# Attention over cached windows on one core: groups of four caches with K stationary, against groups of eight caches with q and P stationary

## The chip, the cores and the metric

One NeuronCore of a Trainium2 chip. The metric is the device time of one execution, in microseconds (us). Unless a range is given, a time is the median of the runs. "Fast" and "slow" are states of a run: a run more than 1.5% above the fastest of its kernel counts as slow, and a single run of a kernel has the state "unknown". TensorE is PE in the profile (its weight loads: PEld), VectorE DVE, ScalarE ACT, GpSimd POOL, SyncE SP. The "clock" is the TensorE clock that was granted, 1.0 being full speed.

## The reference

A decode step: layer norm, attention of one new token over the last 1024 keys of a cache, and a gated FFN whose output multiplies the attention's.

```python
xn = layernorm(x)                                   # x: [8, 1, 512] bf16
q  = (xn @ wq) -> [8, 32 heads, 1, 128]             # wq: [512, 4096]
k  = repeat(k_cache[:, :, 3072:4096], 4)            # caches: [8, 8 kv heads, 4096, 128]
v  = repeat(v_cache[:, :, 3072:4096], 4)
p  = softmax(q @ k^T * 128**-0.5)
s  = (p @ v) @ wo                                   # wo: [4096, 512]
g  = silu((gelu(xn @ w_gate) * (xn @ w_up)) @ w_down)   # F = 1792
out = x + s * g
```

There are 64 windows (8 batches by 8 kv heads) of 256 KB for K and as many for V: 33.6 MB. The weights bring the bytes read to 47.5 MB. The output is so close to x that a wrong order of keys passes the comparison with the reference; only wrong softmax sums failed it (relative error 0.03).

## The kernel before

A group is 4 caches of one kv head (a cache: the window of one batch). K comes as a 1 MB tile: partition 4r+i holds rows of cache i, 8 KB (32 keys) each, with r from 0 to 31. PE transposes K in blocks of 8, VectorE copies the block to SBUF, and K^T is the stationary operand for the scores (the one that the weight loads, PEld, read; the other is the moving one), so that the scores stand with the keys on partitions and 16 query columns beside them. An exp per cache i masks the rows of the other caches through its bias. V is stationary for the values.

```python
I = 4; R = 128 // I; C = 1024 // R                  # 4 caches, 32 rows, 32 keys a row
def load_cache(src, g):
    t = slot()                                      # ring of 21 slots of [128, 8 KB]
    rows = src[b0 : b0 + I, hkv, win0:Sk, :].rearrange("i (r c) d -> r i (c d)", c=C)
    nc.sync.dma_start(out=t, in_=rows)
...
# score_block, 8 of these, N = 16:
nc.tensor.matmul(sc[g][:, s * CB + c, :], kT[n][:, c * P : (c + 1) * P], qT_all[:, hkv, b0 : b0 + I, :], ...)
# once per group, 4 exps of 128 elements a partition:
for i in range(I):
    nc.scalar.activation(out=pT[g][:, :, i * rep : (i + 1) * rep],
                         in_=sc[g][:, :, i * rep : (i + 1) * rep],
                         func=ACT.Exp, bias=diag[:, i : i + 1], scale=inv_sqrt_dh)
# sums by a matmul with ones and a reduction on VectorE; values, 32 of these, N = 16:
nc.tensor.matmul(oT[g], v_t[g][:, c * Dh : (c + 1) * Dh], pT[g][:, c, :], ...)
```

(The load order is K0, w_q, then K and V in turn, FFN, w_o.)

The softmax here doesn't subtract the row's maximum and nothing guards it: scores larger than these inputs give would overflow.

Of the kernel before, what the change touches and what calls it, by code (L numbers as in the profile page):

```python
# [7 lines left out]
ACT = mybir.ActivationFunctionType  # L8
ALU = mybir.AluOpType
AX = mybir.AxisListType  # L10
BF16 = mybir.dt.bfloat16
# [4 lines left out]
def kernel(  # L16
# [13 lines left out]
    nc = tc.nc  # L30
# [14 lines left out]
    I = 4  # L45
    R = P // I
    C = W // R
    NG = Hkv * B // I
    GPH = B // I
    IR = I * rep  # L50
    CB = 8
    NB = C // CB
    SLOT = C * Dh
# [9 lines left out]
    ring = ctx.enter_context(tc.tile_pool(name="ring", bufs=21))  # L63
    consts = ctx.enter_context(tc.tile_pool(name="consts", bufs=1))
    persist = ctx.enter_context(tc.tile_pool(name="persist", bufs=1))
    kT_pool = ctx.enter_context(tc.tile_pool(name="kT_pool", bufs=4))
    p_pool = ctx.enter_context(tc.tile_pool(name="p_pool", bufs=3))
    small = ctx.enter_context(tc.tile_pool(name="small", bufs=3))
    ps_kT = ctx.enter_context(tc.tile_pool(name="ps_kT", bufs=3, space=bass.MemoryType.PSUM))
    ps_sc = ctx.enter_context(tc.tile_pool(name="ps_sc", bufs=2, space=bass.MemoryType.PSUM))  # L70
    ps_m = ctx.enter_context(tc.tile_pool(name="ps_m", bufs=2, space=bass.MemoryType.PSUM))
    ps_s = ctx.enter_context(tc.tile_pool(name="ps_s", bufs=1, space=bass.MemoryType.PSUM))
# [8 lines left out]
    def slot():  # L81
        return ring.tile([P, SLOT], BF16, name="slot")

    k_t, v_t, wo_t = {}, {}, {}
    wq_t, wg_t, wu_t, wd_t = [], [], [], []

    def load_cache(src, g):
        t = slot()
        hkv, b0 = g // GPH, (g % GPH) * I
        rows = src[b0 : b0 + I, hkv, win0:Sk, :].rearrange("i (r c) d -> r i (c d)", c=C)  # L90
        nc.sync.dma_start(out=t, in_=rows)  # L91
        return t
# [6 lines left out]

    def load_wq():  # L100
        for k in range(NDC):
            t = slot()
            nc.sync.dma_start(out=t, in_=A_wq[k * P : (k + 1) * P, :])  # L103
            wq_t.append(t)

    def load_ffn():
        for dst, src in ((wg_t, B_w_gate), (wu_t, B_w_up)):
            for a in range(2):
                t = slot()
                nc.sync.dma_start(  # L110
                    out=t[:, 0 : 2 * F],
                    in_=src[a * 2 * P : (a + 1) * 2 * P, :].rearrange(
                        "(p k) f -> p (k f)", k=2
                    ),
                )
                dst.append(t[:, 0 : 2 * F].rearrange("p (k f) -> p k f", k=2))
        JH = JF // 2
        wd = B_w_down.rearrange("(p j) d -> p j d", j=JF)
        for a in range(2):
            t = slot()[:, 0 : JH * D].rearrange("p (j d) -> p j d", j=JH)  # L120
            nc.sync.dma_start(out=t, in_=wd[:, a * JH : (a + 1) * JH, :])
            wd_t.extend(t[:, j, :] for j in range(JH))

# [20 lines left out]
    for m in range(NM):  # L144
# [9 lines left out]
    ones_pp = consts.tile([P, P], BF16, name="ones_pp")  # L154
    nc.vector.memset(ones_pp, 1.0)
# [3 lines left out]
    sel = consts.tile([P, R, I], FP32, name="sel")  # L159
    nc.gpsimd.memset(sel, 0.0)  # L160
    nc.gpsimd.affine_select(
        out=sel, in_=sel, compare_op=ALU.not_equal, fill=1.0, base=0,
        pattern=[[-I, R], [-1, I]], channel_multiplier=1,
    )
    diag = consts.tile([P, I], FP32, name="diag")
    nc.vector.tensor_reduce(
        out=diag, in_=sel.rearrange("p r i -> p i r"), axis=AX.X, op=ALU.add
# [30 lines left out]
    xq_sb = persist.tile([P, P], BF16, name="xq_sb")  # L198
    nc.gpsimd.memset(xq_sb, 0.0)
    for q in range(NQ):  # L200
        nc.scalar.dma_start(
            out=xq_sb[32 * q : 32 * q + B, :], in_=x_flat[:, q * P : (q + 1) * P]
        )


# [22 lines left out]
    s_ps = ps_s.tile([P, P], FP32, name="s_ps")  # L228
    nc.vector.memset(s_ps, 0.0)

    def transpose_x():
        t = ps_m.tile([P, 2, NDC, B], BF16, name="m_ps")
        for k in range(NDC):
            nc.tensor.transpose(t[:, 0, k, :], xhat[:, k * P : (k + 1) * P], ident[0:B, 0:B])  # L234
        xp = xhat.rearrange("b (a p k) -> b a k p", a=2, k=2)
        for a in range(2):
            for k in range(2):
                nc.tensor.transpose(t[:, 1, 2 * a + k, :], xp[:, a, k, :], ident[0:B, 0:B])
        nc.vector.tensor_copy(out=xnT_sb[:, :, 0:B], in_=t[:, 0])
        nc.vector.tensor_copy(out=xpT_sb[:, :, 0:B], in_=t[:, 1])  # L240


    def project_q():
        NW = rep * Dh
        q_sb = persist.tile([P, Hkv // NQ, NW], BF16, name="q_sb")
        q_ps = [ps_m.tile([P, NW], FP32, name="m_ps") for n in range(Hkv // NQ)]
# [28 lines left out]
    kT, sc, pT, oT = {}, {}, {}, {}  # L275

    def transpose_block(n):
        g, s = n // NB, n % NB
        t_ps = ps_kT.tile([P, CB * P], BF16, name="kT_ps")
        for c in range(CB):  # L280
            cc = s * CB + c
            nc.tensor.transpose(  # L282
                t_ps[:, c * P : (c + 1) * P], k_t[g][:, cc * Dh : (cc + 1) * Dh], ident
            )
        kT[n] = kT_pool.tile([P, CB * P], BF16, name="kT")
        nc.vector.tensor_copy(out=kT[n], in_=t_ps)  # L286

    def score_block(n):
        g, s = n // NB, n % NB
        hkv, b0 = g // GPH, (g % GPH) * I  # L290
        if s == 0:
            sc[g] = ps_sc.tile([P, C, IR], FP32, name="sc_ps")
        for c in range(CB):
            nc.tensor.matmul(  # L294
                sc[g][:, s * CB + c, :],
                kT[n][:, c * P : (c + 1) * P],
                qT_all[:, hkv, b0 : b0 + I, :],
                start=True,
                stop=True,
            )  # L300
        if s == NB - 1:
            pT[g] = p_pool.tile([P, C, IR], BF16, name="pT")
            for i in range(I):
                nc.scalar.activation(  # L304
                    out=pT[g][:, :, i * rep : (i + 1) * rep],
                    in_=sc[g][:, :, i * rep : (i + 1) * rep],
                    func=ACT.Exp,
                    bias=diag[:, i : i + 1],
                    scale=inv_sqrt_dh,
                )  # L310

    recip = {}

    def sum_group(g):
        sums_ps = ps_m.tile([P, C, IR], FP32, name="m_ps")
        nc.tensor.matmul(sums_ps, ones_pp, pT[g], start=True, stop=True)  # L316
        sums = small.tile([P, IR], FP32, name="sums")
        nc.vector.tensor_reduce(  # L318
            out=sums, in_=sums_ps.rearrange("p c m -> p m c"), axis=AX.X, op=ALU.add
        )  # L320
        recip[g] = small.tile([P, IR], FP32, name="recip")
        nc.vector.reciprocal(out=recip[g], in_=sums)  # L322

    def value_block(g, s):
        if s == 0:
            sum_group(g)
            oT[g] = ps_m.tile([P, IR], FP32, name="m_ps")
        for c in range(s * CB, (s + 1) * CB):
            nc.tensor.matmul(  # L329
                oT[g],  # L330
                v_t[g][:, c * Dh : (c + 1) * Dh],
                pT[g][:, c, :],
                start=(c == 0),
                stop=(c == C - 1),
            )
        if s == NB - 1:
            hkv, b0 = g // GPH, (g % GPH) * I
            nc.vector.tensor_tensor(  # L338
                out=oT_all[:, hkv * rep : (hkv + 1) * rep, b0 : b0 + I].rearrange(
                    "p j i -> p i j"  # L340
                ),
                in0=oT[g].rearrange("p (i j) -> p i j", i=I),
                in1=recip[g].rearrange("p (i j) -> p i j", i=I),
                op=ALU.mult,
            )

    oE, wide_t = {}, {}
# [32 lines left out]
    def project_out(m):  # L380
        for e in range(HS):
            for q in range(NQ):
                nc.tensor.matmul(  # L383
                    s_ps[32 * q : 32 * q + B, :],
# [11 lines left out]
    def ffn_up():  # L396
        gu_ps = [ps_m.tile([P, JQ * P], FP32, name="m_ps") for w in range(2)]
        for w, wt in enumerate((wg_t, wu_t)):
            for k in range(NDC):
                cols = wt[k // 2][:, k % 2, :].rearrange("x (p j) -> x j p", j=JF)  # L400
# [30 lines left out]
    def ffn_down():  # L431
        f_ps = ps_m.tile([P, P], FP32, name="m_ps")
        nc.vector.memset(f_ps, 0.0)
        for j in range(JF):
            r = j // JQ
            for q in range(NQ):
# [3 lines left out]
                    wd_t[j][:, q * P : (q + 1) * P],  # L440
# [12 lines left out]
    LA, LAG = 2, 6  # L453
    N = NG * NB
    transpose_x()
    for n in range(LA):
        transpose_block(n)
    project_q()
    for n in range(N + LAG):
        if n + LA < N:  # L460
            transpose_block(n + LA)
        if n < N:
            score_block(n)
        if n >= LAG:
            g, s = (n - LAG) // NB, (n - LAG) % NB
            value_block(g, s)
            GM = HS // rep * GPH
            if g % GM == 0 and g > 0:
                if s == 0:
                    expand_out(g // GM - 1)  # L470
                if s == 3:
                    select_out(g // GM - 1)
# [10 lines left out]
    nc.vector.tensor_tensor(out=tmp, in0=s_ps, in1=g_sb, op=ALU.mult)  # L483
# [37 lines left out]
```

## Time and profile before

| | before |
|---|---|
| time, median of 4 runs | 123.24 us (123.22 to 123.33) |
| span of the profiled run | 121.1 us |
| DMA rate in the slices of the loop | 414 to 434 GB/s |
| PE, DVE, ACT busy | 71%, 60%, 19% |
| mean clock | 0.85 |

The first lines are from the profile page before: the span, busy time with shares and instruction counts, then the span cut in 40 slices (DMA: busy tenths of the 16 engines; GB/s: what they moved).

```profile
span 121.1 us, 4123 instructions
PE 86.0 (71%) x1856; PEld 71.1 (59%) x1856; DVE 72.3 (60%) x150; ACT 22.6 (19%) x70; POOL 2.4 (2%) x15
...
DMA  3999999999999999999999999999999999999820
GB/s 84 387 430 430 430 427 417 419 430 425 425 427 427 425 414 422 430 419 430 425 427 422 422 417 430 422 425 422 425 433 418 422 414 434 416 430 423 341 88 5
```

DMA is at 9 tenths in all slices but the first and the last three; over the span, no compute engine is above 71%. The queue lines of the page (packets, MB, share of 16 engines' span) and its chain of work that ended last say the same:

```profile
q1 hardware_dynamic: 6800, 47.46, 93.7%
q8 instruction: 14, 0.23, 0.7%
...
DMA 82%; PE 12%; DVE 2%; SPq 1%; issue 0%
```

The chain is 82% DMA; the 14 packets of queue q8 are instruction fetches. In the packet records of the trace (a packet is one record of what a DMA engine moved), a packet of 8192 bytes takes 309 ns (median). From the groups (busy us, mean ns; then idle time before them and its releaser):

```profile
L286 DVE COPY kT<-kT_ps 128x1024 bf16<-128x1024 bf16 x64 | 42.2, 677 | 18.1 <-PE kT_ps L282 17.5
L304 ACT ACTIVATE pT<-sc_ps,diag 128x128 bf16<-128x128 f32 x64 | 18.2, 368 | 70.6 <-PE sc_ps L294 70.6
```

The exps take 18.2 us in all. The mean of 368 ns contains overlap; in the timeline four exps take 1.14 us, with starts about 255 ns apart.

### The profile page before, as it was taken

How to read it: one execution, taken by the hardware profiler on the slowest of the kernel's cores; microseconds unless marked ns; L12 is line 12 of the kernel's file. 1: busy time of each engine (PE TensorE's matmuls, PEld its weight loads, DVE VectorE, ACT ScalarE, POOL GpSimd, SP SyncE). 2: the span in 40 equal slices, each digit the busy share in tenths (PEclk: the TensorE clock that was granted, in tenths of full speed). 3: DMA queues.
4: the chain of work that ended last, by engine and by line, in shares of the span. 5: the costliest groups of instructions: out<-in, count | busy, mean ns of one | idle time of the engine just before them, and what ended most of it. 6: DMA issues, size and time to landing. Idle time of an engine off the chain costs nothing.

```text
span 121.1 us, 4123 instructions
## 1 busy us (share of the span) xinstructions
PE 86.0 (71%) x1856; PEld 71.1 (59%) x1856; DVE 72.3 (60%) x150; ACT 22.6 (19%) x70; POOL 2.4 (2%) x15
## 2 busy tenths in 40 slices
PE   0075269696875968999997969566798789955450
PEld 0061029586865957999896969565698542134340
DVE  2352046866956749678989987747798670562000
ACT  0440000321303301212330330303033300300000
POOL 6100000000000000000000000000000000000000
PEclk9999756999999985559999999999999756995555
DMA  3999999999999999999999999999999999999820
GB/s 84 387 430 430 430 427 417 419 430 425 425 427 427 425 414 422 430 419 430 425 427 422 422 417 430 422 425 422 425 433 418 422 414 434 416 430 423 341 88 5
DMA packets 6929, 47.73 MB, mean 394 GB/s; under 512 B 888, under 2 KB 896, under 8 KB 1920
## 3 DMA queue, kind: packets, MB, share of 16 engines
q1 hardware_dynamic: 6800, 47.46, 93.7%
q8 instruction: 14, 0.23, 0.7%
q10 hardware_dynamic: 112, 0.02, 0.1%
q14 instruction: 3, 0.02, 0.1%
HBM read 47.46 MB, written 0.01 MB: 392 GB/s over the span
## 4 chain that ended last, share of the span: by engine, by line
DMA 82%; PE 12%; DVE 2%; SPq 1%; issue 0%
DMA slot<-in_A_k_cache_dram 44%; DMA slot<-in_B_w_gate_dram 16%; DMA slot<-in_A_wo_dram 15%; DMA slot<-in_A_wq_dram 7%; PE kT_ps L282 7%; PE m_ps L329 2%; PE sc_ps L294 2%; SPq L91 1%; PE s_ps L383 1%; DVE kT L286 1%; PE m_ps L316 1%; DVE sums L318 1%; SPq L103 0%; PE m_ps L370 0%; DVE tmp L483 0%
## 5 line engine op out<-in xcount | busy, mean ns | idle before, releaser
L286 DVE COPY kT<-kT_ps 128x1024 bf16<-128x1024 bf16 x64 | 42.2, 677 | 18.1 <-PE kT_ps L282 17.5
L282 PE MATMUL kT_ps<-ident,slot 128*128 128x128 bf16 x512 | 43.4, 234 | 9.9 <-DMA slot<-in_A_k_cache_dram 9.5
L282 PEld LDWEIGHTS <-slot 128*128 128x128 bf16 x512 | 32.6, 104 | 13.3 <-DMA slot<-in_A_k_cache_dram 10.1
L304 ACT ACTIVATE pT<-sc_ps,diag 128x128 bf16<-128x128 f32 x64 | 18.2, 368 | 70.6 <-PE sc_ps L294 70.6
L294 PE MATMUL sc_ps<-qT_all,kT 128*128 128x16 bf16 x512 | 22.9, 171 | 0.3 <-issue 0.3
L329 PE MATMUL m_ps<-pT,slot 128*128 128x16 bf16 x512 | 21.8, 170 | 1.2 <-issue 1.1
L329 PEld LDWEIGHTS <-slot 128*128 128x128 bf16 x512 | 18.6, 97 | 4.6 <-issue 3.1
L294 PEld LDWEIGHTS <-kT 128*128 128x128 bf16 x512 | 20.4, 99 | 0.0
L318 DVE TENSOR_REDUCE sums<-m_ps 128x16 f32<-128x512 f32 x16 | 10.9, 684 | 1.2 <-PE m_ps L316 1.2
L402 PE MATMUL m_ps<-slot,xpT_sb 128*32 128x512 bf16 x32 | 7.7, 1105 | 0.0
L316 PE MATMUL m_ps<-pT,ones_pp 128*128 128x512 bf16 x16 | 6.7, 416 | 0.7 <-ACT pT L304 0.7
L250 PE MATMUL m_ps<-slot,xnT_sb 128*32 128x512 bf16 x32 | 3.5, 527 | 4.2 <-DMA slot<-in_A_wq_dram 4.2
L234 PE MATMUL m_ps<-ident,xhat 8*128 8x8 bf16 x4 | 0.3, 168 | 7.0 <-DVE xhat L214 7.0
L259 DVE CAST q_sb<-m_ps 128x512 bf16<-128x512 f32 x2 | 1.3, 686 | 6.6 <-PE m_ps L250 6.6
L356 DVE TENSOR_TENSOR wide<-m_ps,hmask 64x1024 bf16<-64x1024 bf16 x4 | 4.9, 1216 | 0.5 <-PE m_ps L352 0.4
L483 DVE TENSOR_TENSOR tmp<-s_ps,g_sb 128x128 f32<-128x128 f32 x1 | 0.3, 292 | 7.1 <-PE s_ps L383 7.1
L250 PEld LDWEIGHTS <-xnT_sb 128*32 128x32 bf16 x32 | 0.8, 101 | 6.2 <-issue 5.8
L322 DVE RECIPROCAL recip<-sums 128x16 f32<-128x16 f32 x16 | 4.0, 253 | 0.6
L234 PEld LDWEIGHTS <-xhat 8*128 8x128 bf16 x4 | 0.2, 102 | 7.0 <-DVE xhat L214 7.0
L402 PEld LDWEIGHTS <-xpT_sb 128*32 128x32 bf16 x32 | 1.7, 117 | 4.3 <-issue 3.4
L338 DVE TENSOR_TENSOR oT_all<-m_ps,recip 128x16 bf16<-128x16 f32 x16 | 3.5, 218 | 0.4 <-PE m_ps L329 0.3
L352 PE MATMUL m_ps<-ident,oT_all 128*64 128x128 bf16 x4 | 1.0, 253 | 2.7 <-DVE sums L318 2.1
(71 smaller groups left out, 33.4 us busy)
## 6 DMA issues: line engine op xcount, KB each, us to landing
slot<-in_A_k_cache_dram SPq DMA_DIRECT2D x16, 1024.0 KB, 19.4
slot<-in_A_v_cache_dram SPq DMA_DIRECT2D x16, 1024.0 KB, 19.7
slot<-in_A_wq_dram SPq DMA_DIRECT2D x4, 1024.0 KB, 8.6
slot<-in_A_wo_dram SPq DMA_DIRECT2D x3, 1024.0 KB, 18.0
slot<-in_B_w_gate_dram SPq DMA_DIRECT2D x2, 896.0 KB, 20.0
slot<-in_B_w_up_dram SPq DMA_DIRECT2D x2, 896.0 KB, 18.9
slot<-in_B_w_down_dram SPq DMA_DIRECT2D x2, 896.0 KB
slot<-in_A_wo_dram SPq DMA_DIRECT2D x1, 768.0 KB, 17.7
```

The costliest lines, as they stand in the source:

```text
L250: nc.tensor.matmul(q_ps[n][Q * q : Q * (q + 1), :], xnT_sb[:, k, :], wq_t[k][:, hkv * NW : (hkv + 1) * NW], start=(k == 0), stop=(k == NDC ...
L282: nc.tensor.transpose(t_ps[:, c * P : (c + 1) * P], k_t[g][:, cc * Dh : (cc + 1) * Dh], ident)
L286: nc.vector.tensor_copy(out=kT[n], in_=t_ps)
L294: nc.tensor.matmul(sc[g][:, s * CB + c, :], kT[n][:, c * P : (c + 1) * P], qT_all[:, hkv, b0 : b0 + I, :], start=True, stop=True,)
L304: nc.scalar.activation(out=pT[g][:, :, i * rep : (i + 1) * rep], in_=sc[g][:, :, i * rep : (i + 1) * rep], func=ACT.Exp, bias=diag[:, i : ...
L316: nc.tensor.matmul(sums_ps, ones_pp, pT[g], start=True, stop=True)
L318: nc.vector.tensor_reduce(out=sums, in_=sums_ps.rearrange("p c m -> p m c"), axis=AX.X, op=ALU.add)
L322: nc.vector.reciprocal(out=recip[g], in_=sums)
L329: nc.tensor.matmul(oT[g], v_t[g][:, c * Dh : (c + 1) * Dh], pT[g][:, c, :], start=(c == 0), stop=(c == C - 1),)
L338: nc.vector.tensor_tensor(out=oT_all[:, hkv * rep : (hkv + 1) * rep, b0 : b0 + I].rearrange("p j i -> p i j"), in0=oT[g].rearrange("p (i j ...
L356: nc.vector.tensor_tensor(out=wide, in0=t_ps.rearrange("p (q e) -> p e q", e=HS) .unsqueeze(2) .to_broadcast([HS * B, HS, HS, DQ]), in1=hm ...
L402: nc.tensor.matmul(gu_ps[w][Q * q : Q * (q + 1), :], xpT_sb[:, k, :], cols[:, j0[q] : j0[q] + JQ, :], start=(k == 0), stop=(k == NDC - 1), ...
```

## The change

The intent: fewer, larger transfers and fewer instructions. A group becomes all 8 caches of a kv head, a slot 2 MB with rows of 16 KB, so packets and their fixed cost (9 ns each by the fit in the prediction) halve. Scores keep q stationary (32 columns) and stream K^T as the moving operand in four column tiles (four matmuls, with their outputs in partitions 0 to 31, 32 to 63 and so on); P then stands with queries on partitions, and VectorE transposes it in 32x32 blocks; P is stationary for the values. The sums come from the exps' accumulator outputs, and the ones-matmul with its reduction goes. A half group is half of a K slot and half of a V slot, 1 MB each: the bytes of one group before.

```diff
-    I = 4
+    I = B                                   # 8 caches: R = 16 rows of 16 KB
...
-    ring = ... bufs=21                      # slots of 8 KB a partition
+    ring = ... bufs=8                       # slots of 16 KB a partition
-    ps_sc = ... bufs=2 ;  ps_m = ... bufs=2
+    ps_sc = ... bufs=1 ;  ps_o = ... bufs=2 ;  ps_m = ... bufs=1
...
-        rows = src[b0 : b0 + I, hkv, win0:Sk, :].rearrange("i (r c) d -> r i (c d)", c=C)
+        rows = src[:, g, win0:Sk, :].rearrange("i (r c) d -> r i (c d)", c=C)
         nc.sync.dma_start(out=t, in_=rows)
...
+    def score_unit(h):                      # a half group: 2 x 4 matmuls, N = 512
+                nc.tensor.matmul(sc_ps[Q * kb : Q * (kb + 1), a], qT_all[:, g]...,
+                                 kT[2 * h + a][:, :, Q * kb : Q * (kb + 1)], ...)
+        src = sc_ps.rearrange("p a c (r i) -> p (a c r) i", i=I)
+        dst = p_sb[h].rearrange("p (n i) -> p n i", i=I)
+        for i in range(I):                  # 8 exps of 128 elements a partition
+            nc.scalar.activation(out=dst[:, :, i], in_=src[:, :, i], func=ACT.Exp,
+                                 bias=diag[:, i : i + 1], scale=inv_sqrt_dh,
+                                 accum_out=acc[g][:, u, i : i + 1])
+    def turn_unit(h):
+        nc.vector.transpose(out=pT[h]..., in_=p_sb[h])           # 128x1024 in 32x32 blocks
+    def value_part(h, part, nparts):        # 4 parts of 4 matmuls, N = 256, two column tiles
+            nc.tensor.matmul(o_ps[g][64 * (z % 2) : 64 * (z % 2 + 1), :], pT[h][:, 2 * y : 2 * y + 2, :]...,
+                             v_t[g][:, 2 * z * Dh : (2 * z + 2) * Dh], ...)
...
+    # sum_group: matmul of acc with `same`; scale_group on ScalarE; close_group: fold, copy to oT_all
+    # w_q, FFN and w_o are loaded as 2 MB (1.75 MB) slots; s_ps is zeroed late, in project_out(0)
```

## The prediction

> **What bounds it now.** The DMA stream. In the page's 40 slices DMA is 9 tenths busy nearly throughout, at 414 to 434 GB/s; queue q1 moves 47.46 MB and takes 93.7% of 16 engines' span; the chain that ended last is 82% DMA. PE (71%), VectorE (60%) and ScalarE (19%) have slack; the loop ends at 98.7 us (timeline), the FFN hides behind the last loads. The tail: the last big w_o piece lands at 116.7 us, 32 matmuls take 1.05 us, two VectorE operations 0.6 us.
>
> In the DMA packet records, 8192-byte packets take 309 ns, 7168: 272, 2048: 84, that is 9 ns plus 36.6 ns per KB. The 14 instruction-fetch packets of 16 KB take 935 ns each and slow a neighbour. The engines land the first load within 0.4 us of each other, the last 3 us apart (window 114 to 117 us: DMA share 0.54, 0.39, 0.30). Steps of 1.4 us come with the fetches, seemingly rotating over 8 engines: the slowest carry two.
>
> **DMA after.** Rows of 16 KB halve the packets: 376 per engine become about 192, estimate 184 x 9 ns = 1.7 us, and 21 fewer loads save 0.2 us. PE instructions fall from about 3700 to 2400, so about 9 fetches remain instead of 14[...]: no engine carries two, 1.4 us less at the slowest. DMA should end 3.2 us earlier. Given back: the last w_o tile is now 64 matmuls, 56 of them after the second-last landing, about 1 us more tail. Net of the DMA path: -2.3 us.
>
> **Compute.** Per half group (a 2 MB load, about 4.85 us): PE 32 transposes 1.8 us, 8 score matmuls about 0.6 (as the q projection in four column tiles), 16 value matmuls about 0.9. VectorE: 3.5 copies of 0.68[...], small things 0.3: 3.9 us.
>
> ScalarE is the danger: 8 exps (257 ns apart today, 2.2 us for 8) plus an unknown accumulator read, every second half a 1 us copy of kT, and only one score buffer, so scores(h+1) wait for exps(h). In odd halves PE's fourth block waits for that copy, behind the exps. Estimated cycle: exps plus 1.6 us. With a 0.1 us read 4.7 us, just hidden; with 0.15 5.1; with 0.2 5.5, 5 us late. Scores start about 2.5 us later (21.5 against 18.9): 6 MB must land first, not 5. I expect loop end near 100.5 and the w_o work just compute-bound (s_ps is now zeroed after the FFN gate), costing 1 us.
>
> **Prediction: 122.0 us** (120.0 to 126.5). Chances: faster over 2% 0.22, within 2% 0.56, slower over 2% 0.22.
>
> **Right if:** big packets number about 3070, 16 KB ones near 609 ns; DMA at 430 GB/s or more, last landing near 113.5; PE's waits before score matmuls name ScalarE exps; tail of 64 matmuls about 2 us.
>
> **Wrong if:** 16 KB rows are cut in 8 KB packets (no gain), or eight sources 8 MB apart slow reads; accumulator reads cost over 0.15 us each, so exps take over 3.4 us per half and ScalarE paces the run (slower by 3 to 8%); the PE clock drops to 0.5 with the new waits; or reads are so cheap that the DMA path alone decides (near 121.0).

The 9 fetches stand as an estimate in proportion to PE's instructions (14 x 2400 / 3700 = 9.1). The other was VectorE's term for the transpose: what is left, 3.5 copies of 0.68 and 0.3, comes to 2.7 us, and the rest of the 3.9 us is the cut term. The forecast itself: 123.24 less 2.3 for DMA plus 1 for the w_o work is 121.9.

What the trace before shows for other terms. A load also has 16 packets of 4 bytes at 9 ns, one an engine if they are spread evenly, so 21 fewer loads come to 0.2 us. Packets of 8192 bytes beside a fetch took 774 to 855 ns in place of 309. The 16 landings of a load spread over 0.3 to 0.5 us before the first fetch, over 1.6 to 1.9 after it and over 3.0 to 3.4 from the ninth on: these are the steps of 1.4 us. Eight transposes take 0.62 us and one alone 0.22, so a further one 57 ns: 32 come to 1.8, and 16 matmuls of 256 columns in two column tiles, if both run at once, to 0.9. On ScalarE 128 elements take 277 ns and 512 take 597, so 1024 come to 1.02 us, an estimate for the copy of kT. A clock of 0.5 is in the page before, too (from 15 to 20, 46 to 52 and 112 to 121 us).

## The result, and the profile after

205.1 us (204.47 to 207.02, 4 runs) against 123.24. The ratio of the fast runs is 1.667, with a 95% interval of 1.656 to 1.678. (A ratio is the mean time of one kernel's fast runs over that of the other's of the same rounds, so not quite the ratio of the medians.) The range of the prediction ended at 126.5.

The same lines of the page after the change:

```profile
span 203.2 us, 3061 instructions
PE 118.3 (58%) x1246; PEld 76.0 (37%) x1246; DVE 74.4 (37%) x129; ACT 90.8 (45%) x278; POOL 4.7 (2%) x24
...
DMA  6999999999999999999999999999999999999000
GB/s 156 207 362 413 310 206 219 239 213 210 248 213 208 224 232 210 213 216 235 213 213 219 235 213 221 232 216 210 216 229 223 206 247 440 426 431 412 36 3 2
...
q1 hardware_dynamic: 3488, 47.45, 92.0%
q8 instruction: 9, 0.15, 0.3%
...
PE 31%; DMA 25%; ACT 20%; another core or an unknown queue 10%; DVE 10%; issue 2%; SPq 0%; DVEq 0%; ACTq 0%
```

DMA is as busy as before, 9 tenths in nearly every slice, but moves only half as much: 206 to 248 GB/s while caches are loaded (slices 6 to 33), and 412 to 440 for FFN and w_o after that. The count of packets did fall, from 6800 to 3488, and the instruction fetches from 14 to 9, as intended. Busy is not the same as fast: a share of busy time alone would have called this stream healthy. Nor does the chain name it: it puts PE first, with 31%, and DMA at 25%. The packet records give the reason for the low rate, by what is loaded:

| packets | bytes | median ns |
|---|---|---|
| before, caches | 8192 | 309 |
| after, w_q and w_o | 16384 | 611 |
| after, K and V caches | 16384 | 1196 to 1246, by load |
| after, FFN | 14336 | 535 |

The packets of the caches take twice as long as packets of the same size to the same tile from w_q. At 220 GB/s the 33.6 MB of caches take 153 us, at 424 GB/s 79 us: that difference, 73 us, is most of the 82 us lost (an estimate from these two rates).

What each engine did in the window from 60 to 80 us, before and after (busy us, with instruction counts; then clock, DMA share and GB/s):

```profile
core 0: us, PE busy (x) PEld busy (x) DVE busy (x) ACT busy (x) POOL busy (x), PEclk, DMA share, GB/s
...
60.00:80.00 20.00, 15.54 (x397) 14.54 (x395) 15.62 (x32) 4.56 (x16) 0.00 (x0) 1.00 1.01 424
```

```profile
60.00:80.00 20.00, 10.00 (x89) 6.63 (x86) 6.98 (x12) 9.12 (x30) 0.00 (x0) 0.66 1.02 222
```

PE fell from 15.5 to 10.0 busy us of 20 and from a clock of 1.00 to 0.66. So PE waits more. The waits of PE (us in total, times, longest) and the costliest groups after the change:

```profile
PE kT_ps L283 <- DMA slot<-in_A_k_cache_dram: 39.9, 8, 8.4
PE sc_ps L299 <- ACT p_sb L313: 11.3, 8, 1.9
PE m_ps L348 <- DVE oT_all L370: 4.9, 5, 1.3
```

```profile
L313 ACT ACTIVATE p_sb<-sc_ps,diag 128x128 bf16<-128x128 f32 x128 | 77.2, 1030 | 70.5 <-PE sc_ps L299 70.5
L313 ACT ACTIVATION_READ_ACCUMULATOR p_sb<-sc_ps,diag 128x1 f32 x128 | 65.4, 511 | 0.0
L324 DVE STREAM_TRANSPOSE pT<-p_sb 128x1024 bf16<-128x1024 bf16 x16 | 19.8, 1236 | 7.7 <-ACT p_sb L313 7.7
```

Two more costs are visible behind the DMA. The exps (L313) took 18.2 us before and take 77.2 us now, and the timeline has their starts about 0.57 us apart, in place of 0.255. Each also has a read of the accumulator, 511 ns in the records. The transpose on VectorE took 1236 ns.

So the theories at this point were: for the loads, (A) the eight sources, 8 MB apart; (B) the long rows; (C) the count of rows or sources; (D) the places in SBUF that are written. For the exps, (E) the accumulator reads, (F) the strided access.

### The profile page after: what moved, and what is told of

It is laid out like the page before. It is cut to its first block, busy times and chain, and to the rows that moved or that the text cites. A ratio compares the mean times of both kernels' runs of the same rounds, so it can differ in the third digit from the quotient of the medians.

```text
span 203.2 us, 3061 instructions
## 1 busy us (share of the span) xinstructions
PE 118.3 (58%) x1246; PEld 76.0 (37%) x1246; DVE 74.4 (37%) x129; ACT 90.8 (45%) x278; POOL 4.7 (2%) x24
## 3 DMA queue, kind: packets, MB, share of 16 engines
q1 hardware_dynamic: 3488, 47.45, 92.0%
## 4 chain that ended last, share of the span: by engine, by line
PE 31%; DMA 25%; ACT 20%; another core or an unknown queue 10%; DVE 10%; issue 2%; SPq 0%; DVEq 0%; ACTq 0%
ACT p_sb L313 19%; DMA slot<-in_A_k_cache_dram 17%; PE kT_ps L283 11%; PE o_ps L334 8%; DMA slot<-in_A_wq_dram 8%; PE sc_ps L299 4%; DVE pT L324 3%; PE m_ps L348 2%; PE o_ps L433 2%; PE o_ps L414 2%; DVE kT L291 2%; DVE wide L384 1%; PE m_ps L468 1%; DVE oT_all L370 1%
## 5 line engine op out<-in xcount | busy, mean ns | idle before, releaser
L313 ACT ACTIVATE p_sb<-sc_ps,diag 128x128 bf16<-128x128 f32 x128 | 77.2, 1030 | 70.5 <-PE sc_ps L299 70.5
L283 PE MATMUL kT_ps<-ident,slot 128*128 128x128 bf16 x512 | 52.1, 270 | 40.3 <-DMA slot<-in_A_k_cache_dram 39.9
L313 ACT ACTIVATION_READ_ACCUMULATOR p_sb<-sc_ps,diag 128x1 f32 x128 | 65.4, 511 | 0.0
L283 PEld LDWEIGHTS <-slot 128*128 128x128 bf16 x512 | 41.2, 123 | 59.2 <-DMA slot<-in_A_k_cache_dram 43.9
L334 PE MATMUL o_ps<-slot,pT 128*64 128x256 bf16 x256 | 31.9, 361 | 0.0
L324 DVE STREAM_TRANSPOSE pT<-p_sb 128x1024 bf16<-128x1024 bf16 x16 | 19.8, 1236 | 7.7 <-ACT p_sb L313 7.7
L299 PE MATMUL sc_ps<-kT,qT_all 128*32 128x512 bf16 x128 | 12.4, 472 | 11.7 <-ACT p_sb L313 11.3
L334 PEld LDWEIGHTS <-pT 128*64 128x64 bf16 x256 | 12.6, 133 | 8.2 <-issue 4.2
L289 ACT COPY kT<-kT_ps 128x1024 bf16<-128x1024 bf16 x8 | 10.4, 1296 | 9.6 <-PE kT_ps L283 9.6
L367 PE MATMUL m_ps<-pick,o_sb 128*128 128x32 f32 x32 | 7.5, 370 | 3.8 <-ACT o_sb L360 3.8
L299 PEld LDWEIGHTS <-qT_all 128*32 128x32 bf16 x128 | 2.8, 99 | 15.5 <-issue 14.8
```

What stands on the lines that cost most here:

```text
L283: nc.tensor.transpose(t_ps[:, c, :], k_t[g][:, cc * Dh : (cc + 1) * Dh], ident)
L289: nc.scalar.copy(out=dst, in_=t_ps)
L299: nc.tensor.matmul(sc_ps[Q * kb : Q * (kb + 1), a], qT_all[:, g].rearrange("p b j -> p (b j)"), kT[2 * h + a][:, :, Q * kb : Q * (kb + 1)] ...
L313: nc.scalar.activation(out=dst[:, :, i], in_=src[:, :, i], func=ACT.Exp, bias=diag[:, i : i + 1], scale=inv_sqrt_dh, accum_out=acc[g][:, u ...
L324: nc.vector.transpose(out=pT[h].rearrange("p c m -> p (c m)"), in_=p_sb[h])
L334: nc.tensor.matmul(o_ps[g][64 * (z % 2) : 64 * (z % 2 + 1), :], pT[h][:, 2 * y : 2 * y + 2, :].rearrange("p c m -> p (c m)"), v_t[g][:, 2 ...
```

## The experiments

The kernel before ran beside them at 123.1 to 123.3 us (medians). The runs of sections 1 to 6 are single ones, of unknown state; the differences that are read from them are large, or within one trace.

### 1. p1_sources: loads alone, the source varied

Twelve stages of three 2 MB loads (6 MB), each ended by a read of the tile (the two stages with 8 KB rows: six loads of 1 MB). Nothing is computed; the output is x by construction. "16 x 8" is the pattern of a load: an outer count of 16 rows, and for each of them 8 sources.

```python
("contiguous",          [[8 * ROW, 16], [ROW, 8], [1, ROW]]),   # ROW = 16 KB
("eight_8MB",           [[ROW, 16], [BP, 8], [1, ROW]]),        # the change's pattern
("eight_8MB_less_4KB",  [[ROW, 16], [BP - ROW // 4, 8], [1, ROW]]),
("four_8MB_32_rows",    [[ROW, 32], [BP, 4], [1, ROW]]),        # and so on
```

> Loads alone, wrong result on purpose: twelve stages, each three loads of 2 MB into the same tile, that differ only in where the rows come from. Theory A (sources): rows of eight caches whose addresses agree modulo 8 MB are read at the same time by different DMA engines and get in each other's way. Then the contiguous stage runs near 430 GB/s (packets of 16 KB about 611 ns), eight sources 8 MB apart near 220 GB/s (about 1200 ns), the same with the pitch cut by 256 KB near 430, with the pitch cut by 16 KB still slow, four sources x 32 rows of 16 KB near 430, two sources x 64 rows near 430, four sources with 8 KB rows (as in the kernel before) near 425, eight sources with 8 KB rows still near 220. Theory B (long strided packets): 16 KB packets are slow whenever the rows are not one piece, so every strided 16 KB stage is near 220 and both 8 KB stages are near 425. The pitches of 4, 2 and 1 MB are open[...].

| stage: rows x sources | pitch of sources | us for 6 MB | GB/s | median packet, ns |
|---|---|---|---|---|
| contiguous, 128 rows of 16 KB | | 16.0 | 393 | 611 |
| 16 x 8 of 16 KB | 8 MB | 28.8 | 218 | 1227 |
| 16 x 8 of 16 KB | 8 MB less 4, 16, 256 KB | 29.6 to 29.7 | 212 to 213 | 1253 to 1272 |
| 16 x 8 of 16 KB | 4, 2, 1 MB | 29.6 | 212 to 213 | 1253 to 1262 |
| 32 x 4 of 16 KB | 8 MB | 15.6 | 403 | 611 |
| 64 x 2 of 16 KB | 8 MB | 15.9 | 397 | 611 |
| 32 x 4 of 8 KB | 8 MB | 15.6 | 402 | 309 |
| 16 x 8 of 8 KB | 8 MB | 26.9 | 234 | 594 |

The pitch changes nothing, so A falls. Long rows are fast in 32 x 4 and short rows slow in 16 x 8, so B falls (short rows help a little: 234 GB/s in place of 218). What is slow is an outer count of 16 with 8 sources, from wherever.

### 2. e1_half_rows, e2_shifted, e3_shifted_no_sums: the same in the kernel

```diff
 # e1: two loads of 8 KB rows per slot, still 16 x 8
+for a in range(2): cut = slice(a * SLOT // 2, (a + 1) * SLOT // 2)
+    nc.sync.dma_start(out=t[:, cut], in_=rows[:, :, cut])
 # e2: sources 8 MB less 256 KB apart (other keys, wrong on purpose)
+pitch = Hkv * Sk * Dh - R * SLOT
+rows = bass.AP(src.tensor, (g * Sk + win0) * Dh, [[SLOT, R], [pitch, I], [1, SLOT]])
 # e3: e2 without accum_out, acc set to 1 (wrong on purpose)
```

> The changed kernel with each cache load cut into two loads of 8 KB rows, same sources, same slots. Theory A (sources collide): no better, 195 to 210 us, 8 KB packets near 600 ns. Theory B (long packets): back to about 425 GB/s, and a time set by the ScalarE cycle, 130 to 145 us.

> The changed kernel with 16 KB rows and eight sources, but each further source starts 256 KB lower in its cache (wrong keys and values on purpose), so no two rows of a load agree modulo 8 MB. Theory A: packets near 611 ns, the stream above 420 GB/s while it is fed; the time is then set by ScalarE (8 exps with their accumulator reads at 0.575 us each, 4.6 us, plus about 1.6 us for scores, kT copy and the fourth block, per half group): 132 to 145 us. Theory B: unchanged, near 205 us.

> The run before this one without the accumulator outputs of the exps (sums set to one, wrong on purpose). If the accumulator reads are the second cause, ScalarE needs about 2.2 us for 8 exps, the cycle falls to about 3.9 us, under the 4.85 us of a 2 MB load, and the time is that of the DMA stream with its tail: 119 to 124 us. If something else paces the half group (the single score buffer, PE waits, PE clock), it stays above 130 us.

Measured, one run each: 192.05, 209.51 and 204.76 us. The packets of e1 (8 KB) took about 560 ns, at about 235 GB/s; those of e2 about 1230 ns. None is near 130 us. So in the kernel, too, A and B fall; rows of 8 KB alone are worth 13 us. e3 was wrong, and its ScalarE was still busy for 90.5 us: hidden behind DMA, this run could not tell E from F.

### 3. p2_destinations: loads alone, the partitions varied

> Loads alone again, wrong result on purpose, all with rows of 16 KB. The first loads showed that the pitch of the sources does not matter and that 16 rows x 8 sources is slow where 32 x 4 and 64 x 2 are fast. Theory D (destinations):[...] Then 32 x 4 from 32 far caches is fast (about 400 GB/s), 64 x 2 from 64 caches fast, 16 x 8 from nearly one piece slow (about 215), and for 64 partitions filled as 16 x 4 the place decides: partitions 0 to 63 slow, 64 to 127 slow, 32 to 95 fast, with the same sources. Two halves (0 to 63, then 64 to 127) on one queue slow[...]. Two queues: open. Theory S (number of distant sources in flight): 16 x 8 from nearly one piece is fast, the 32 and 64 far caches slow, and the place of 64 partitions makes no difference.

| stage | partitions | us for 6 MB | GB/s |
|---|---|---|---|
| 32 x 4, sources far apart | 0 to 127 | 15.9 | 395 |
| 16 x 8, nearly one piece of memory | 0 to 127 | 30.3 | 208 |
| 64 x 2, sources far apart | 0 to 127 | 16.1 | 391 |
| 16 x 8, sources 8 MB apart, as in p1 | 0 to 127 | 29.3 | 215 |
| 16 x 4 | 0 to 63 | 30.5 | 206 |
| 16 x 4 | **32 to 95** | **15.7** | **402** |
| 16 x 4 | 64 to 127 | 30.8 | 205 |
| 16 x 4 twice, one queue | 0 to 63, 64 to 127 | 29.6 | 213 |
| 16 x 4 twice, two queues | 0 to 63, 64 to 127 | 28.4 | 222 |
| 8 x 4 first, then the halves (6.8 MB) | 0 to 31, then as above | 32.3 | 211 |

The very same load is twice as fast when it is written 32 partitions further on. So it is the place that decides: theory D. The last stage, with a load of 8 x 4 first to put the rows out of step, was expected to be fast; it did not help (211 GB/s), and that expectation failed.

### 4. p3_engines, p4_home, p5_one_pair: which rows meet

How many packets of a load are under way at once follows from rate x packet time / packet size, with the figures of the table below: 7.7 for 8 x 4 (207 GB/s x 611 ns / 16384 bytes), 3.8 for 4 x 4, 1.9 for 2 x 4, 8.3 for 9 x 4 at 32, 11.3 for 12 x 4 at 32, 15.1 for 16 x 4 at 32; for 16 x 8 in p1 it is 16.3. So up to 16 it is about one packet for each outer row. Which rows get in each other's way was a hypothesis of mine that fits p2: two outer rows written 32 partitions apart, both within 0 to 63 or both within 64 to 127 (a pair). In the fast stage of p2, 32 to 95, the rows that are 32 apart lie on the two sides of partition 64, and there is no pair. In a 16 x 8 load a row is 8 partitions, 0 to 7, 8 to 15 and so on, and every row is in a pair. These three runs test that.

```python
# loads alone; (name, loads, first partition, partitions, source)
("16x4_to_16", 6, 16, 64, [[ROW, 16], [BP, 4], row]),   ("12x8_to_0", 4, 0, 96, [[ROW, 12], [BP, 8], row])
("8x4_to_16",  6, 16, 32, [[ROW, 8], [BP, 4], row]),    ("9x4_to_0",  6, 0, 36, [[ROW, 9], [BP, 4], row])
```

> Loads alone (the result is junk on purpose), rows of 16 KB, about 6 MB in each stage, to find how an outer count of 16 loses half the rate. Theory:[...] Then: 32x4 and 16x4 into partitions 32 to 95 about 400 GB/s with 611 ns packets; 16x8 about 215 GB/s, all packets near 1225 ns; 16x4 into partitions 16 to 79: half of the packets near 1225 ns and half near 611 (partitions 16 to 31 meet 48 to 63, the others meet nobody), so about 215 GB/s at the end but bimodal; 12x8 into 0 to 95: two thirds near 1225 and one third near 611[...]; 12x8 into 32 to 127: the same thirds; 8x16 in natural order:[...] near 1225 ns and 110 GB/s or worse. Rival: an outer count of 16 or less is slow in itself, whatever the partitions: then 16x4 into 16 to 79 and both 12x8 have one kind of packet and no fast share.

> Loads alone again (junk on purpose), rows of 16 KB with four sources, six loads a stage[...]. Theory 1, sharing (damaged by the stages of 16x4 at 16 and of 12x8, which had no fast packets): every stage has packets near 611 ns. Theory 2,[...] 8x4 at 0 and at 32, 4x4 at 0 and 2x4 at 0 near 611 ns, 8x4 at 16, 64 and 96, 4x4 at 16 and 64, 2x4 at 8 and 64 near 1220 ns. Theory 3, a small outer count is slow in itself: all but 16x4 at 32 near 1220 ns.

> Loads alone (junk on purpose), rows of 16 KB with four sources.[...] 8x4 at 0, no shared pair: near 611 ns, 207 GB/s. 9x4 at 0, one more row, one shared pair (0 to 3 with 32 to 35): if the pair holds back all, nearly all packets are near 1225 ns and the rate FALLS to about 120 GB/s; if only the pair suffers, two ninths of the packets are near 1225 ns and the rest near 611. 9x4 at 32 (no pair): 611 ns, about 230 GB/s. 9x4 at 28 (one pair, 28 to 31 with 60 to 63): as 9x4 at 0. 12x4 at 0 (four pairs): near 1225 ns and 155 GB/s; 12x4 at 32 (no pair): 611 ns and 305 GB/s. If 9x4 at 28 or at 0 is fast, sharing is not it.

(How a load is shared out over the engines and why two rows meet, no trace shows. "Sharing" is the hypothesis of the pairs; theory 2 of p4 was that some places are slow whatever else is written.)

| run | stage | pairs 32 apart | GB/s | packets |
|---|---|---|---|---|
| p3 | 32 x 4; 16 x 4 at 32 | not counted; none | 393; 406 | 611 ns |
| p3 | 16 x 8 at 0 | all 16 | 210 | 1278 ns |
| p3 | 16 x 4 at 16 | 8 rows of 16 | 214 | nearly all about 1230 ns |
| p3 | 12 x 8 at 0; at 32 | 8 rows of 12 | 162; 162 | nearly all 1000 to 1300 ns |
| p3 | 8 x 16 at 0 | all 8 | 111 | about 1130 ns |
| p4 | 8 x 4 at 0, 16, 32, 64, 96 | none | 204 to 208 | 611 ns (medians here and below) |
| p4 | 4 x 4 at 0, 16, 64; 2 x 4 at 0, 8, 64 | none | 101 to 103; 51 to 53 | 611 ns |
| p5 | 8 x 4 at 0 | none | 207 | 611 ns |
| p5 | **9 x 4 at 0** | one pair | **121** | 2 of 9 slow (48 of 216), most others 611 ns |
| p5 | 9 x 4 at 32 | none | 223 | 611 ns |
| p5 | 9 x 4 at 28 | one pair | 118 | 2 of 9 slow, most others 611 ns |
| p5 | 12 x 4 at 0; at 32 | four pairs; none | 160; 304 | 1240 ns; 611 ns |

(Pairs by the hypothesis; the trace does not record which engine carried a packet, nor to which row it belonged. A load of 32 outer rows is not counted: it was fast in p1 to p3, 393 to 403 GB/s, and the hypothesis covers up to 16 rows.) Every stage without a pair had packets of 611 ns, whatever its count or start; the rivals of p4, a slow place and a small outer count, fall. One more row, 9 x 4 for 8 x 4, took a stage from 207 to 121 GB/s, and two ninths of its packets (the share of two rows of nine) were slow (over 1200 ns). Moved by 32 partitions, the same load was fast. So these runs fit that the two rows of a pair take twice as long and the load ends with them (36 packets at 121 GB/s take 4.9 us, as long as four of 1220 ns in a row). In a 16 x 8 load all rows are in pairs, and nearly all of its packets were slow (median 1227 ns in p1, 1278 in p3).

One thing is not explained: in stages with four pairs, also the rows that meet none were slow (16 x 4 at 16, 12 x 4 at 0, 12 x 8). For p3 I had expected fast and slow packets side by side there; what came is what its rival, a small outer count, foretold; but 16 x 4 at 32, fast in the same run, and p4 exclude that rival. With one pair the others were not slow. What couples them stays open; it does not touch the 16 x 8 load, where all rows are in pairs.

### 5. e4_four_sources, e5_four_sources_no_sums: the loads mended

```diff
-rows = src[:, g, win0:Sk, :].rearrange("i (r c) d -> r i (c d)", c=C)
-nc.sync.dma_start(out=t, in_=rows)
+for u in range(NU):                               # two loads of 32 x 4 rows of 8 KB
+    rows = src[4 * u : 4 * u + 4, g, win0:Sk, :].rearrange("i (r c) d -> r i (c d)", c=CU)
+    nc.sync.dma_start(out=t[:, u * CU * Dh : (u + 1) * CU * Dh], in_=rows)
 # e5: as e4, accum_out taken away, acc set to 1 (wrong on purpose)
```

The compute is left as it was, so the masks do not fit the new order of caches: e4 is wrong too.

> The changed kernel with its 2 MB slots filled as in the kernel before, by two loads of 32 rows x 4 caches of 8 KB (keys end up under other masks, wrong on purpose); all compute as changed. Packets near 309 ns, stream above 420 GB/s when it is fed. If ScalarE is the second cause (8 exps with accumulator reads 4.6 us, cycle about 6.2 us per half group): 130 to 145 us, PE waiting for exps before scores. If DMA was the only cause: 119 to 124 us.

> The run before this one without accumulator outputs. If the reads are what ScalarE pays: 119 to 124 us (8 exps 2.2 us, cycle about 3.9 us). If the single score buffer, PE or its clock pace the loop instead: above 128 us.

e4 took 162.46 us, e5 161.6 (one run each). I had expected 130 to 145 us for e4. Packets are back at 310 ns, and the rate is at 421 to 435 GB/s in slices 8 to 24. The new loads are worth 43 us of the 82, not the 73 of the estimate, since other costs come up from behind them. They differ from the old ones in rows of 8 KB as well as in shape; against e1, which has these rows in the old shape, the shape alone is worth 30 us. From the page of e4, the GB/s row, the chain and the exps:

```profile
GB/s 154 433 415 444 407 425 427 427 427 421 425 423 427 423 427 429 427 423 429 427 423 425 435 429 421 43 252 430 308 36 385 105 0 4 0 0 0 4 0 2
...
PE 36%; ACT 34%; DVE 14%; DMA 10%; issue 3%; SPq 1%; DVEq 0%; ACTq 0%
...
L314 ACT ACTIVATE p_sb<-sc_ps,diag 128x128 bf16<-128x128 f32 x128 | 77.4, 1031 | 31.2 <-PE sc_ps L300 31.2
```

DMA leads the chain no more (10%), and its row breaks off to 43 GB/s in slice 26: loads wait for free slots. ScalarE's share is now 34%. Without accumulators (e5) the time and the exps are the same, eight exps in 4.82 us. So E falls here: the reads cost nothing measurable (161.6 against 162.46 us). In the records each read ends with its own exp, within 4 ns, so its 511 ns are not work on top. That is shown for results 16 bytes apart; no run has the reads together with packed results.

### 6. e6_packed_writes, e7_packed_reads: the exps

```diff
 # e6: e5, results side by side
-dst = p_sb[h].rearrange("p (n i) -> p n i", i=I)
+dst = p_sb[h].rearrange("p (i n) -> p n i", i=I)
 # e7: e5 (dst as there), reads side by side
-src = sc_ps.rearrange("p a c (r i) -> p (a c r) i", i=I)
+src = sc_ps.rearrange("p a c q -> p (a c q)").rearrange("p (i n) -> p n i", i=I)
```

> The version with the two four-source loads and no accumulators (161.6 us, eight exps in 4.82 us), but each exp writes its 128 results side by side; it still reads every eighth element of PSUM (wrong on purpose: P is in the wrong order). If the strided write to SBUF (16 bytes apart) is what makes an exp 0.60 us, eight exps now take 2.1 to 2.6 us (0.26 to 0.32 each) and the time falls to about 138 us. If the strided read from PSUM (32 bytes apart) does it, nothing changes: 4.8 us and 161 us.

> The mirror image: each exp reads 128 neighbouring elements of PSUM and still writes every eighth element of SBUF (wrong on purpose). If the read makes an exp 0.60 us, eight exps now take 2.1 to 2.6 us and the time is about 138 us; if the write does, 4.8 us and 161 us. If both runs change little, each of the two strides alone suffices; if both give about half, their costs add.

e6 took 142.54 us, e7 160.79 (one run each, both wrong). ScalarE's timeline between 60 and 66 us, e5 and then e6 (start, us, what):

```profile
59.76 4.82 ACT L315 ACTIVATE p_sb<-sc_ps,diag 128x128 bf16<-128x128 f32 x8
```

```profile
63.66 2.18 ACT L315 ACTIVATE p_sb<-sc_ps,diag 128x128 bf16<-128x128 f32 x8 [6.60 <-PE sc_ps L300]
```

The strided write to SBUF does it all: 2.18 us for eight exps in place of 4.82, with the read from PSUM still at every eighth element; the starts are 0.25 us apart in place of 0.57. In e7 the reverse changed nothing. The writes were 16 bytes apart: 0.57 us from start to start for 128 elements is 4.5 ns for each. The four exps of the next run write 256 elements 8 bytes apart, over the same 2 KB, and start 0.61 us apart: 2.4 ns for each element, about half as much, and 4.8 ns for each 16 bytes of the stretch written. They have their accumulator reads back, so this second figure fits a cost by the stretch but does not show it.

### 7. c1_four_exps: right by construction

Each half slot now holds the four caches of its load, so four exps of 256 elements, 8 bytes apart, do a half group.

```diff
+    IL = I // NU                                   # e4 and:
-        src = ... "p a c (r i) -> p (a c r) i", i=I ;  for i in range(I):  bias=diag[:, i : i + 1]
+        src = ... "p a c (r i) -> p (a c r) i", i=IL ; for i in range(IL): bias=diag[:, u * IL + i : u * IL + i + 1]
```

> A correct version: two loads of 32 x 4 rows of 8 KB per slot, so each half group holds only four caches, and four exps of 256 elements with accumulators do instead of eight of 128. Estimate per half group 4 x (0.257 + 0.107 + 0.31) = 2.7 us of ScalarE, cycle about 4.3 us, hidden under 4.88 us of DMA. Fewer instruction fetches than in the kernel before (9 against 14) end the slowest DMA engine about 1.4 us earlier, the longer tail gives about 1 us back: 121 to 124 us.

(The 0.107 us is for 128 elements more, by the 277 ns for 128 elements and 597 for 512 in the trace before; 0.31 is 0.57 less 0.257.)

138.85 us (138.54 to 140.95, 4 runs); ratio to before 1.126 (1.124 to 1.129). The expectation failed. DMA was done in the first 115 us, and its chain share is 30%. PE now leads with 45%.

### 8. c1a_two_value_parts, c1b_close_first, c2_fewer_switches: the order on PE and VectorE

Two suspects were left in c1, seen among PE's and its weight loads' waits: the short stops ("issue") of the first weight load after a change between value, score and transpose matmuls, and a wait for the single small PSUM buffer.

```profile
PE m_ps L350 <- DVE oT_all L372: 6.5, 5, 1.7
```

```profile
PEld L285 <- issue: 15.1, 49, 0.8
```

```diff
 # c1a: values in two parts of 8 instead of four of 4
+if a % 2 == 1: value_part(v, a // 2, TB // 2)
 # c1b: close_group(g - 1), with its copy on VectorE, ahead of turn_unit; sum_group in the odd half
+if a == 1 and v > 0 and v % NU == 0: close_group(v // NU - 1)
 if a == 1 and 0 < h <= NH: turn_unit(h - 1)
 # c2: both
```

> The four-exps version (138.9 us) with only the value matmuls in two parts per half instead of four. If the switches of the tile mode are most of what the version with both edits gained (7 to 10 us), this gives 131 to 134 us; if the wait for the small PSUM buffer is, 136 to 138 us.

> The four-exps version with only the other edit: the copy of finished outputs ahead of the 1.24 us transpose and the sums moved to the odd half, values still in four parts. If the wait for the small PSUM buffer (6.5 us) is most of what the version with both gained, 132 to 134 us; if the switches are, 136 to 138 us.

> The correct version with four exps (138.9 us) with three changes of order: the value matmuls in two parts per half instead of four, the copy of the finished outputs ahead of the 1.24 us transpose on VectorE, and the sums moved to the odd half. Theory: the rest over before is PE, by[...] the wait for the one small PSUM buffer (6.5 us), of which some hides under other waits: 126 to 132 us. Rival: PE is bound by the lower clock and by the late FFN and w_o tail: 136 to 139 us.

| | all runs, us | fast runs, us |
|---|---|---|
| c1 | 138.54 to 140.95 | 138.5 to 139.0 (3) |
| c1a | 136.07 to 141.62 | 136.1, 137.5 (2) |
| c1b | 131.48 to 133.99 | 131.5 to 133.2 (3) |
| c2 | 128.47 to 132.82 | 128.5 (1) |

I had put most on the changes of mode: about 10 us of c2's forecast. c1's trace has 49 stops at L285 with 15.1 us in all, 0.31 us each. The fast runs say otherwise: fewer changes alone give 1 to 3 us, the other edit 5 to 7.5. That one moves both the copy and the sums, and the two were not separated. The copy had stood behind a transpose of 1.24 us, while PE could not have the only m_ps buffer. In c1b that wait is gone (its trace is of a slow run, 133.99 us), and what PE waits for is the cache again. In c1a the wait is still there:

```profile
PE kT_ps L285 <- DMA slot<-in_A_k_cache_dram: 6.6, 5, 2.4
```

```profile
PE m_ps L350 <- DVE oT_all L372: 6.9, 5, 1.8
PEld L285 <- issue: 9.3, 25, 0.8
```

With only one fast run, c2's step beyond c1b is not secured.

### 9. c3_ffn_first, b1_before_ffn_first: the tail

c2's trace is of a slow run (132.82 us); the fast one was not profiled. Its window after the last loads, and its chain, show DMA finished near 115 us and then nearly 16 us of work, the FFN first. Two pieces of that chain (start, us, what), the last values of the loop and the FFN's matmuls:

```profile
110.00:115.00 5.00, 4.61 (x24) 0.88 (x27) 2.59 (x2) 0.36 (x1) 0.00 (x0) 0.70 0.83 348
```

```profile
107.91 1.08 PE o_ps L336 x16
...
110.85 3.77 PE o_ps L435 x16
```

c3 loads the FFN's weights after K1 and computes the FFN ahead of the second pair of half groups (the zeroing of s_ps moves, too; cut below). b1 does the same to the kernel before, as a control.

```diff
-    load_k(0); load_wq(); for g in range(1, NG): load_k(g); load_v(g - 1)  ...  load_ffn()
+    load_k(0); load_wq(); load_k(1); load_ffn(); load_v(0); for g in range(2, NG): load_k(g); load_v(g - 1) ...
+        if h == NU: ffn_up(); ffn_down()
+    close_group(NG - 1); expand_out(1); project_out(0); select_out(1); project_out(1)
```

> The last version (131.8 us) with the FFN's weights loaded and the FFN computed ahead of the loop over the caches, the zeroing of the output's PSUM tile early, and the first half of the output projection under the expansion of the second. In that version DMA was done about 113 us into the span and 17 us of compute followed, of which the FFN's chain was some 13. If that tail was what was left, DMA still ends near 114 and the span is 118 to 121 us: 120 to 123 us, that is level with or up to 2.5% faster than before. Rival: the compute loop itself is late by more than the 9.5 us that the last w_o loads take, then 125 to 129 us.

> A control: the kernel before with the same move of the FFN. There the FFN already hides behind the last loads and DMA decides, so the move alone should give nothing: 122.5 to 124 us. If it gains as much as it gains in the other kernel, the order of loads is a gain of its own and says nothing of the change.

c3: fast runs 130.1 to 130.3 us, slow ones to 134.6; ratio of fast runs 1.058 (1.056 to 1.060). That is no faster than the one fast run of c2 (128.5). b1: 122.95 us, ratio 0.999 (0.998 to 1.000): the move by itself gives nothing. My expectation for c3 failed and the rival held: with the FFN out of the tail the loop itself ended later. Its last value matmuls in the chain of c3:

```profile
116.49 1.08 PE o_ps L338 x16
```

They end at 117.6 us, some 2 us after the last bytes, and another 7.8 us of short steps in a row (fold, expansion, selection, the last 64 w_o matmuls, two VectorE operations) end at 125.3; in the kernel before, most of these had long been done under the loads, since its last value matmuls ended at 97.9 us. In c3 the FFN's weights come before the caches, so the last cache bytes land at 105.5 us in place of 92.7 in c2. From these bytes to the last value matmuls it is 12.1 us in c3 (a fast run), 16.3 in c2 (109.0), 3.7 before. So in c2 and c3 DMA is as quick as before, a little quicker, and the compute of the loop ends late.

The mean, 5.5 us for each half group in c2 (87.7 us over 16, from the scores' start at 21.3 us) against 4.9 for each group of the same bytes before (78.9 us over 16, from 19.0), hides where. By the starts of the scores, the first ten half groups of c2 take 4.7 us each, about what the loads take (2.1 MB at 427 GB/s: 4.9 us); the next five take 6.7 in c2 and 5.9 in c3, against 5.1 before. In this stretch of both, PE waits once for the only m_ps buffer behind a 2.25 us VectorE operation, the first `wide` of the output's expansion, and once behind oE (1.7 us). From the waits of PE in c2:

```profile
PE m_ps L350 <- DVE wide L386: 4.1, 1, 4.1
```

This is the same kind of wait as the one behind the transpose, which c1b removed; this one c1b has, too. What it costs was not tested: no run takes it away. In the same stretch the granted clock is 0.5 for some microseconds at a time, and 16 transposes then take 1.8 us in place of 1.0 (from 83.3 and from 74.5 us in c2). No version beat the kernel before.

## Why the prediction was wrong

- **DMA after.** The terms of counts were right: 3072 packets of 2 KB or more where "about 3070" was said, 9 instruction fetches where "about 9" was said (14 before), 611 ns for 16 KB where w_q and w_o are concerned. **The step that failed is "16 KB ones near 609 ns", taken from the line of 9 ns plus 36.6 ns per KB** (of 1000 bytes): for the caches it was 1196 to 1246 ns, and so the stream ran at 206 to 248 GB/s in place of "430 GB/s or more". The line had been read from loads such as 32 x 4 rows, and in 16 x 8 rows the same size takes twice as long (611 and 1227 ns in p1). I had looked at the size of the packets and not at where the rows are written. The prediction named "eight sources 8 MB apart slow reads" as a danger, and the number to watch was well chosen, but the cause was not the sources (runs p1, e2).
- **The gain that was meant.** Part of it exists, once the load is mended. In c2 the last w_o packet lands 113.0 us after the first big packet, before 114.8 (b1: 114.6; packet records): 1.6 to 1.8 us earlier, against 3.2 predicted. c2 keeps packets of 8 KB for the caches; what of this comes from fewer fetches and what from larger weight packets was not separated. No run of the whole kernel had 16 KB cache rows in a shape that was fast in p1, so the gain that was meant stays untested as a whole.
- **ScalarE.** "257 ns apart today, 2.2 us for 8" was mis-sized: 4.8 us in the changed kernel (77.2 us over 16 half groups). The accumulator read, named as the danger, cost nothing measurable (161.6 us in e5 against 162.46 in e4). What cost was the write at 16 bytes' stride, which the prediction did not look at; the 2.2 us is what e6 measured (2.18) with packed writes. That ScalarE would pace the run if exps exceeded 3.4 us per half was right, as e5 and e6 show (161.6 and 142.5 us); the 3 to 8% foretold for it was too small, since e4 is 32% slower than before.
- **PE.** The three PE terms, 3.3 us per half together, were near for the full clock: in the chain of c2, 32 transposes take 2.0 us there, 8 score matmuls 0.55 and 16 value matmuls 1.1, together 3.7. At a granted clock of 0.5 the same trace has 3.6, 1.0 and 2.0. Left out were the waits and stops: the wait for the single m_ps buffer behind the 1.24 us transpose (with the sums, c1b: 5 to 7.5 us in all) and the stops at changes of mode (c1a: 1 to 3 us). The mean clock fell to 0.72 after the change; in c2 it is 0.88, no lower than before (0.85).
- **VectorE.** For the transpose 1236 ns was measured, and with it the other terms come to the 3.9 us foretold. (The page before has another VectorE operation with 1024 elements a partition, `wide`, at 1216 ns.)
- **The sum.** Undone one after the other: loads (shape and row length) 205.1 to 162.5 us, exps 162.5 to 138.7, order 138.7 to 128.5 (fast runs; for the last there is one alone). The rest to 123.2 is a loop whose last value matmuls end about 11 us later than before (109.0 against 97.9 us in the two traces, that of c2 being slow), which moving the FFN did not mend. That last part is located, in the last five half groups; its cause is not tested.

The chances stood at 0.22 for slower; the error was larger than a range built from known sizes could hold, since a packet time was carried over to a load of another shape.

## What to carry to other kernels

Before a load is reshaped, work out which partitions its rows are written to at the same time: one pair of rows 32 partitions apart took a load from 207 to 121 GB/s (p5), and GB/s tells this where the busy share does not (9 tenths at 206 to 248 GB/s). Write results side by side, even if the read must stride (0.25 us for an exp in place of 0.57, e6). A cost behind the bottleneck is invisible until the bottleneck goes, so sum the busy time of every engine over the new time, and look for single buffers that wait behind one long instruction.
